# Tap products of two steps made together, signal products behind the inverse ones, and four store rooms instead of six

## The chip, the cores and the metric

The kernel runs on one core of a Trainium2 chip. The metric is the device time of one execution in microseconds (us); below it is given as the median of a few runs, with their spread.

## The reference

Two branches work on the same input x of 2048 rows and 512 columns, and a gate mixes them. All of it is fp32.

```python
g = sigmoid((x * gate_w).sum(-1, keepdims=True))
K = einsum("dn,dnl,dn->dl", C, exp(dt * A * l), dt * B).real   # taps, 512 x 2048
y = irfft(rfft(pad(x)) * rfft(pad(K)))[:, :2048] + x * Dskip   # long convolution
b = gelu(x @ w1 + b1) @ w2 + b2                                # 512 -> 1792 -> 512
out = g * y + (1 - g) * b
```

## The kernel before

The program has two parts. The function `front` makes the gate, nearly all of the dense branch b and the first stage of two Fourier transforms, that of the signal x and that of the taps K; a planner with a table of due times sets its order. Its results lie in DRAM (`tu_d` for the signal, `tk_d` for the taps, `od` for the dense branch) and in rooms in SBUF. The change does not touch `front`.

The function `conv`, which the change edits, runs from about 399 us of the span to its end. Its order is written out by hand: each engine does its instructions in the order of the program. Its loop has 16 steps; step s treats the two rows of frequencies 2s and 2s+1.

- `taps(s)` (line 1283 through `pair`): second stage for the taps, two products with 128 rows and 64 columns of weights into each of two PSUM banks, `pk0` and `pk1`. ScalarE then copies each bank into a room `k` (line 1291). There is one bank of each name, so that the next `taps` waits for the copies.
- `signal(s)` (also line 1283): the same for the signal, with weights of 64 rows and 64 columns, into two of four banks `pu0` to `pu3`.
- `product(s)` (lines 1305 to 1310): six VectorE operations multiply the two spectra, from the `pu` banks and the `k` rooms into `v`.
- `inverse(s)` (line 1322): the inverse transform's first stage, again with 64 by 64 weights, into the banks `pa0` and `pa1`, of which there is one each.
- `turn(s)` (lines 1328 to 1330): ScalarE copies `pa0` and `pa1` into two of the store rooms `sa`, and SyncE's queue stores these in DRAM (`t_d` in the profile). After each fourth step, GpSimd's queue loads the turned data of four steps back (line 1342); where a load's target is still in use it is held and issued later (line 1411).
- `fetch(n)` (line 1255): SyncE's queue loads a tap row of 256 KB. `consts` (line 1247) loads constants, and `matrices` (lines 1268 and 1269) lets ScalarE make weights `f` from them, four operations in each odd step up to step 11. `dense` (line 1355) loads 512 KB of the dense branch in steps 4 to 8, 10 and 12, and `gated` (line 1361) scales two tiles of it on ScalarE in steps 10 to 15.

In step s, TensorE's order before is: signal(s+1), taps(s+2), inverse(s). Behind the loop stand what is left of the dense branch (`rest`, lines 1372 to 1374) and the last stage (line 1445). In the texts below, T(s), S(s), I(s) and D(s) stand for taps(s), signal(s), inverse(s) and product(s).

Of the kernel before, what the change touches and what calls it, by code (L numbers as in the profile page):

```python
# [17 lines left out]
P = 128  # L18
L = 2048
D = 512  # L20
# [71 lines left out]
N_ATTIC, N_LOFT, N_TK = 11, 8, 8  # L92
# [295 lines left out]
def gated_mix(  # L388
# [37 lines left out]
    def places(attic, loft, den, shed):  # L426

        rooms = [attic[:, k] for k in range(N_ATTIC)] + [loft[:, k * D : k * D + D] for k in range(N_LOFT)]
        return [den[:, k] for k in range(N_DEN)] + rooms + [shed[:, k] for k in range(32 - N_DEN - N_ROOM)]
# [799 lines left out]
    def conv(pool, ps, late, attic, loft, den, shed, io, ahead):  # L1229


        def tiles(n, shape, nm):
            return [pool.tile(shape, F32, name=f"{nm}{k}", bufs=1) for k in range(n)]

        ks, zs = (tiles(n, [P, D], nm) for n, nm in ((4, "k"), (2, "z")))
        f1s = tiles(2, [P, 4, 64], "f1")
        cc3 = tiles(1, [P, 384], "cc")
        g1t = pool.tile([P, 2, 64], F32, name="g1t", bufs=1)
        t3 = tiles(3, [P, 8, D], "t3")
        vs = tiles(4, [P, D], "v")  # L1240
        sas = tiles(6, [P, D], "sa")
        us = places(attic, loft, den, shed)
        ko = k0_order()
        c4s, mats, t2s = {}, {}, {}
# [1 line left out]
        def consts(m):  # L1246
            nc.sync.dma_start(ccs[m % 4], c2[m])
            c4s[m] = ccs[m % 4]

        def fetch(n):  # L1250
            if 16 <= n < 24:
                t2s[n] = t3[0][:, n - 16]
            else:
                t2s[n] = rows[:, n % N_TK]
            nc.sync.dma_start(t2s[n], tk_d[ko[n]])

        def matrices(m):

            cc = c4s[m]
            f = cc[:, 0:256].rearrange("p (n k) -> p n k", n=4)  # L1260
            f1 = f1s[m % 2]
            for a in (0, 64):
                re, im = slice(a, a + 32), slice(a + 32, a + 64)
                if m < 2:
                    nc.gpsimd.tensor_scalar(f1[re], f[im], -1.0, None, ALU.mult)
                    nc.gpsimd.tensor_copy(f1[im], f[re])
                else:
                    nc.scalar.mul(f1[re], f[im], -1.0)
                    nc.scalar.copy(f1[im], f[re])
            mats[m] = (f, f1), cc[:, 256:384].rearrange("p (s k) -> p s k", s=2)  # L1270
# [3 lines left out]
        def pair(s, r, c, out):  # L1274

            for i in range(2):
                n = 2 * s + i
                if r:
                    w, x = mats[n // 4][0][c][:, n % 4], t2s[n]
                else:  # L1280
                    h = slice(64 * c, 64 * c + 64)
                    w, x = mats[n // 4][0][0][h, n % 4], us[n][h]
                nc.tensor.matmul(out[64 * i : 64 * i + 64], w, x, start=True, stop=True)  # L1283

        def taps(s):
            fac[s] = []
            for c in range(2):
                pk = ps.tile([P, D], F32, tag=f"pk{c}", name=f"p2k{s}{c}", bufs=1)
                pair(s, 1, c, pk)
                k = ks[2 * c + s % 2]  # L1290
                nc.scalar.copy(k, pk)
                fac[s].append(k)

        def signal(s):
            pus[s] = []
            for c in range(2):
                pu = ps.tile([P, D], F32, tag=f"pu{2 * (s % 2) + c}", name=f"p2u{s}{c}", bufs=1)
                pair(s, 0, c, pu)
                pus[s].append(pu)

        def product(s):

            (ur, ui), (kr, ki) = pus.pop(s), fac.pop(s)
            v = [vs[2 * i + s % 2] for i in range(2)]
            nc.vector.tensor_mul(v[0], ur, kr)
            nc.vector.tensor_mul(v[1], ur, ki)
            nc.vector.tensor_mul(zs[0], ui, ki)
            nc.vector.tensor_mul(zs[1], ui, kr)
            nc.vector.tensor_sub(v[0], v[0], zs[0])
            nc.vector.tensor_add(v[1], v[1], zs[1])  # L1310
            prod[s] = v

        def inverse(s):

            v = prod.pop(s)
            for i in range(2):
                n = 2 * s + i
                pas[n] = ps.tile([P, D], F32, tag=f"pa{i}", name=f"pa{s}{i}", bufs=1)
                r = slice(64 * i, 64 * i + 64)
                w = mats[n // 4][1][r, s % 2]  # L1320
                for c in range(2):
                    nc.tensor.matmul(pas[n][64 * c : 64 * c + 64], w, v[c][r], start=True, stop=True)  # L1322

        def turn(s):

            for n in (2 * s, 2 * s + 1):
                sa = sas[n % 6]
                nc.scalar.copy(sa, pas.pop(n))
                g, k = divmod(n, GROUP)
                nc.sync.dma_start(t4_d[g, :, k].rearrange("e c q d -> (c q) e d"), sa)  # L1330
                if k < GROUP - 1:
                    continue
                rows = t4_d[g].rearrange("e k c q d -> (e k c) q d")

                for h in (0, 4, 8, 16, 24) if g == 3 else (0, 8, 16, 24):
                    if h > (16, 8, 8, 24)[g]:
                        held.append((t3[h // 8 % 3][g:P:4], rows[:, h : h + 8]))
                        continue
                    on = nc.gpsimd if n < 31 else nc.scalar
                    e = h + (4 if g == 3 and h < 8 else 8)  # L1340
                    to = t3[h // 8 % 3][g:P:4] if h > 7 else den[g:P:4, h:e]
                    on.dma_start(to, rows[:, h:e])
# [4 lines left out]
        def dense(k, on):  # L1347

            q = (*HERE, *THERE).index(k)
            if q < 5:  # L1350
                mos[k] = attic[:, 2 * q : 2 * q + 2]
            else:
                r = 2 * q - 10
                mos[k] = loft[:, r * D : (r + 2) * D].rearrange("p (s d) -> p s d", s=2)
            on.dma_start(mos[k], od[k])

        def gated(k):

            for i in range(2):
                z = mos[k][:, i]  # L1360
                nc.scalar.mul(z, z, gate[:, 1, 2 * k + i : 2 * k + i + 1])

        def rest(n):

            while late and n:
                s, h, l, w, wl = late.pop(0)
                first = s not in accs
                last = not any(e[0] == s for e in late)
                if first:
                    accs[s] = ps.tile([P, D], F32, tag=f"pu{s}" if s > 1 else f"pk{s}", name=f"acc{s}", bufs=1)  # L1370
                ss = slice(s % 2 * P, s % 2 * P + P)
                nc.tensor.matmul(accs[s], h[:, ss], w, start=first, stop=False)  # L1372
                nc.tensor.matmul(accs[s], h[:, ss], wl, start=False, stop=False)
                nc.tensor.matmul(accs[s], l[:, ss], w, start=False, stop=last)
                n -= 1
# [16 lines left out]
        signal(0)  # L1392
        signal(1)
        taps(0)
        taps(1)
        for s in range(16):

            for n in range(2 * s + N_TK + (2 if s else 0), 2 * s + N_TK + 4):
                if n < 24:
                    fetch(n if n < 16 else n + 8)  # L1400
            if s in (2, 4, 6, 8):
                consts(s // 2 + 3)
            if s % 2 and s < 13:
                matrices(s // 2 + 2)
            product(s)
            if 0 < s < 15:
                signal(s + 1)
            if s + 2 < 16:
                taps(s + 2)
            if s in (10, 11, 12):  # L1410
                nc.sync.dma_start(*held.pop(0))
            if s == 15:
                rest(N_REST)
            inverse(s)
            turn(s)
            if s in TIMES:
                dense((*HERE, *THERE)[TIMES.index(s)], nc.sync)
            if s > 9:
                gated(HERE[s - 10])
# [5 lines left out]
        for s in range(4):  # L1425
            m, i = 7 - s // 2, s % 2
            z, g = mos[m][:, i], gate[:, 1, 2 * m + i : 2 * m + i + 1]
# [9 lines left out]
        for k, m in enumerate(ORDER):  # L1437
# [10 lines left out]
            for i in range(2):  # L1448
                t = 2 * m + i
                z, g = mos[m][:, i], gate[:, 0, t : t + 1]  # L1450
# [32 lines left out]
    with (  # L1483
        tc.tile_pool(name="fp", bufs=2, reuse_waits="tile") as fp,
        tc.tile_pool(name="ps_f", bufs=2, space=PSUM, reuse_waits="tile") as ps_f,
    ):
        conv(fp, ps_f, late, attic, loft, den, shed, io, ahead)
# [66 lines left out]
```

## Time and profile before

| what | us |
|---|---|
| median of 3 runs | 495.22 (494.23 to 496.56) |
| the profiled execution, its own time | 495.36 |
| its span, first to last instruction | 493.6 |
| TensorE busy in the span | 481.9 (98%) |
| VectorE busy | 416.2 (84%) |
| ScalarE busy | 368.9 (75%) |

The span is what the trace covers; the time of the same execution is 1.8 us longer. Busy time of TensorE is modelled from pipelined instructions, so a busy TensorE is not one without waits. The granted TensorE clock is 0.998 of full speed over the span.

### The profile page before, as it was taken

Reading aid. Unit: us, or ns where it says so; the run is one execution under the profiler, and the core shown is the slowest. Engines: PE = TensorE matmul, PEld = TensorE weight load, DVE = VectorE, ACT = ScalarE, POOL = GpSimd, SP = SyncE. Lnnn points to the kernel's source line nnn. Section 1 sums busy time; section 2 is a strip of 40 time slices with the busy share of each in tenths; the row PEclk is TensorE's granted clock in tenths of the full one; section 3 lists DMA queues with packets and bytes.
Section 4 is the critical chain, followed back from the end, with each engine's and each line's share of the span. In section 5 each row is a group of like instructions: output and inputs, shape, how many; then the busy total and the mean of one; then the engine's idle time right before and its main releaser. Section 6 shows DMA issues by size and latency. Waiting matters only on the chain.

```text
span 493.6 us, 12103 instructions
## 1 busy us (share of the span) xinstructions
PE 481.9 (98%) x4782; PEld 374.7 (76%) x4782; DVE 416.2 (84%) x653; ACT 368.9 (75%) x686; POOL 66.8 (14%) x107
## 2 busy tenths in 40 slices
PE   8999999999999999999999999999999999999995
PEld 7888787898897898888887979888888943222651
DVE  6999989989999997999899595999981149999563
ACT  4999767899885899996777997577655358789523
POOL 1102020110102100220121101020201040100012
PEclk9999999999999999999999999999999999999999
DMA  8989992686699762999784858695698897999988
GB/s 309 350 298 305 322 207 67 168 247 199 103 241 228 254 154 101 227 280 280 148 194 72 213 118 217 167 224 170 131 287 220 179 318 272 310 404 417 402 269 333
DMA packets 83848, 116.05 MB, mean 235 GB/s; under 512 B 39900, under 2 KB 43504, under 8 KB 83248
## 3 DMA queue, kind: packets, MB, share of 16 engines
q1 hardware_dynamic: 73776, 87.59, 54.8%
q0 software_dynamic: 9152, 23.89, 23.0%
q10 hardware_dynamic: 864, 3.80, 2.4%
q8 instruction: 37, 0.61, 0.5%
q14 instruction: 19, 0.16, 0.1%
HBM read 65.97 MB, written 49.29 MB: 234 GB/s over the span
## 4 chain that ended last, share of the span: by engine, by line
PE 85%; ACT 6%; DVE 6%; issue 2%; POOL 0%; DVEq 0%; ACTq 0%; POOLq 0%
PE pk L837 12%; PE ph L1029 9%; PE acc L1088 9%; PE ph L1031 9%; PE ph L1030 9%; PE acc L1089 8%; PE acc L1090 8%; PE p2k L1283 6%; PE pa L1322 3%; PE pb L1445 3%; PE ph L517 3%; PE p2u L1283 2%; PE pk L1160 1%; PE acc L1372 1%; DVE y L812 1%
## 5 line engine op out<-in xcount | busy, mean ns | idle before, releaser
L1029 PE MATMUL ph<-xh,wh 128*128 128x256 f32 x432 | 123.3, 286 | 2.1 <-issue 1.2
L1031 PE MATMUL ph<-xh,wl 128*128 128x256 f32 x432 | 122.2, 283 | 0.0
L1030 PE MATMUL ph<-xlo,wh 128*128 128x256 f32 x432 | 122.1, 283 | 0.0
L1029 PEld LDWEIGHTS ph<-xh,wh 128*128 128x128 f32 x432 | 82.0, 190 | 8.9 <-issue 4.0
L1030 PEld LDWEIGHTS ph<-xlo,wh 128*128 128x128 f32 x432 | 82.0, 190 | 3.3 <-issue 1.3
L1088 PE MATMUL acc<-wh,hh 128*128 128x512 f32 x206 | 83.2, 404 | 0.1
L1031 PEld LDWEIGHTS ph<-xh,wl 128*128 128x128 f32 x432 | 82.0, 190 | 0.0
L1089 PE MATMUL acc<-wl,hh 128*128 128x512 f32 x206 | 81.1, 394 | 0.3 <-DVE wl L940 0.3
L1090 PE MATMUL acc<-wh,hl 128*128 128x512 f32 x206 | 80.5, 391 | 0.0
L1060 ACT ACTIVATE ph<-ph,b1t 128x256 f32<-128x256 f32 x112 | 50.4, 450 | 34.0 <-PE ph L1031 30.6
L643 DVE TENSOR_TENSOR loft<-den,shed 128x512 f32<-128x512 f32 (+2 forms) x48 | 67.0, 1396 | 0.2
L1073 DVE TENSOR_TENSOR hl<-ph,hh 128x512 fp32r<-128x512 f32 (+1 forms) x62 | 38.2, 618 | 30.2 <-ACT hh L1063 27.4
L837 PE MATMUL pk<-y,den 128*32 128x64 f32 x2048 | 61.6, 290 | 0.2 <-DVE y L823 0.2
L837 PEld LDWEIGHTS pk<-y,den 128*32 128x32 f32 x2048 | 57.2, 136 | 4.1 <-issue 2.2
L1088 PEld LDWEIGHTS acc<-wh,hh 128*128 128x128 f32 x206 | 38.7, 188 | 17.2 <-issue 8.6
L1090 PEld LDWEIGHTS acc<-wh,hl 128*128 128x128 f32 x206 | 38.7, 188 | 8.7
L1089 PEld LDWEIGHTS acc<-wl,hh 128*128 128x128 f32 x206 | 38.7, 188 | 6.4 <-DVE wl L940 0.6
L1063 ACT CAST hh<-ph 128x512 fp32r<-128x512 f32 (+1 forms) x62 | 33.1, 533 | 10.1 <-PE acc L1089 7.3
L644 DVE TENSOR_TENSOR den<-loft 128x256 f32<-128x256 f32 (+2 forms) x48 | 37.2, 775 | 0.2
L812 DVE TENSOR_TENSOR y<-y,loft 128x2048 f32<-128x2048 f32 x16 | 36.6, 2286 | 0.1
L737 DVE CUSTOM_DVE_ANT_0 phase<-phase 128x128 uint16<-128x128 uint16 (+1 forms) x64 | 25.8, 403 | 0.5
L1060 ACT ACT_TABLE_LOAD x20 | 25.7, 1283 | 0.3
(204 smaller groups left out, 862.8 us busy)
## 6 DMA issues: line engine op xcount, KB each, us to landing
tu_d<-attic SPq DMA_DIRECT2D x64, 128.0 KB, 4.7
tk_d<-sk SPq DMA_DIRECT2D x32, 256.0 KB, 5.6
t_d<-sa SPq DMA_DIRECT2D x32, 256.0 KB, 5.7
ahead<-tk_d SPq DMA_DIRECT2D x18, 256.0 KB, 3.7
attic<-in_xt_dram SPq DMA_DIRECT2D x16, 256.0 KB, 5.4
xh_d<-xh SPq DMA_DIRECT2D x8, 512.0 KB, 5.8
xl_d<-xlo SPq DMA_DIRECT2D x8, 512.0 KB, 7.9
attic<-in_xs_dram SPq DMA_DIRECT2D x16, 256.0 KB, 4.9
```

Of the source, the lines that this page charges most:

```text
L643: vec(4 * m, lambda: nc.vector.tensor_mul(t, z, b), due, [ka, "zz"], kt)
L812: v.tensor_mul(y[:, 0].rearrange("p (a b) c -> p a b c", a=2), e.rearrange("p (a b) c -> p a b c", a=2), cc,)
L837: nc.tensor.matmul(pks[q][32 * j : 32 * j + 32, :, gg], x[:, r, :, ch], y[:, r, :, ch], start=(r == 0), stop=(r == 1), skip_group_check=True,)
L1029: nc.tensor.matmul(p, h, xh[xk][:, d], start=(d == 0), stop=False)
L1030: nc.tensor.matmul(p, h, xlo[xk][:, d], start=False, stop=False)
L1031: nc.tensor.matmul(p, lo, xh[xk][:, d], start=False, stop=(d == 3))
L1060: nc.scalar.activation(phs[q][:, n], phs[q][:, n], AF.Gelu_apprx_tanh, bias=b1t[:, f : f + 1])
L1073: nc.vector.tensor_sub(lo, phs[q][:, 0:nf], hi.bitcast(F32))
L1088: nc.tensor.matmul(a, h, wh[1][w], start=start, stop=False)
L1089: nc.tensor.matmul(a, h, wl[1][w], start=False, stop=False)
L1090: nc.tensor.matmul(a, l, wh[1][w], start=False, stop=(j == 3))
L1283: nc.tensor.matmul(out[64 * i : 64 * i + 64], w, x, start=True, stop=True)
```

## The change

In each even step up to step 12 the taps of two steps are made, one behind the other, ahead of that step's inverse product; odd steps make none. The signal product of step s+2 comes behind the inverse product of step s. There are six `k` rooms instead of four, and four `sa` rooms instead of six. Tap rows are loaded four at a time, in steps 0, 2 and 4, the last eight up to two steps sooner. The tiles `t3` change places with `cc` and `g1t`.

```diff
--- before.py
+++ after.py
@@ -1232,13 +1232,13 @@
         def tiles(n, shape, nm):
             return [pool.tile(shape, F32, name=f"{nm}{k}", bufs=1) for k in range(n)]
 
-        ks, zs = (tiles(n, [P, D], nm) for n, nm in ((4, "k"), (2, "z")))
+        ks, zs = (tiles(n, [P, D], nm) for n, nm in ((6, "k"), (2, "z")))
         f1s = tiles(2, [P, 4, 64], "f1")
+        t3 = tiles(3, [P, 8, D], "t3")
         cc3 = tiles(1, [P, 384], "cc")
         g1t = pool.tile([P, 2, 64], F32, name="g1t", bufs=1)
-        t3 = tiles(3, [P, 8, D], "t3")
         vs = tiles(4, [P, D], "v")
-        sas = tiles(6, [P, D], "sa")
+        sas = tiles(4, [P, D], "sa")
         us = places(attic, loft, den, shed)
         ko = k0_order()
         c4s, mats, t2s = {}, {}, {}
@@ -1287,7 +1287,7 @@
             for c in range(2):
                 pk = ps.tile([P, D], F32, tag=f"pk{c}", name=f"p2k{s}{c}", bufs=1)
                 pair(s, 1, c, pk)
-                k = ks[2 * c + s % 2]
+                k = ks[3 * c + s % 3]
                 nc.scalar.copy(k, pk)
                 fac[s].append(k)
 
@@ -1324,7 +1324,7 @@
         def turn(s):
 
             for n in (2 * s, 2 * s + 1):
-                sa = sas[n % 6]
+                sa = sas[n % 4]
                 nc.scalar.copy(sa, pas.pop(n))
                 g, k = divmod(n, GROUP)
                 nc.sync.dma_start(t4_d[g, :, k].rearrange("e c q d -> (c q) e d"), sa)
@@ -1395,24 +1395,28 @@
         taps(1)
         for s in range(16):
 
-            for n in range(2 * s + N_TK + (2 if s else 0), 2 * s + N_TK + 4):
-                if n < 24:
-                    fetch(n if n < 16 else n + 8)
+            if s == 0:
+                for n in range(8, 12):
+                    fetch(n)
             if s in (2, 4, 6, 8):
                 consts(s // 2 + 3)
             if s % 2 and s < 13:
                 matrices(s // 2 + 2)
             product(s)
-            if 0 < s < 15:
-                signal(s + 1)
-            if s + 2 < 16:
+            if s % 2 == 0 and s < 14:
                 taps(s + 2)
+                taps(s + 3)
+                if s in (0, 2, 4):
+                    for n in range(12, 16) if s == 0 else range(2 * s + 20, 2 * s + 24):
+                        fetch(n)
             if s in (10, 11, 12):
                 nc.sync.dma_start(*held.pop(0))
             if s == 15:
                 rest(N_REST)
             inverse(s)
             turn(s)
+            if s < 14:
+                signal(s + 2)
             if s in TIMES:
                 dense((*HERE, *THERE)[TIMES.index(s)], nc.sync)
             if s > 9:
```

The order of TensorE's instructions, from I(8) on (`pa` is written by inverse products, `p2u` by signal products, `p2k` by tap products). Before:

```order
L1322 MATMUL pa_5018<-v_4661,ahead 64x512
L1322 MATMUL pa_5018<-v_4663,ahead 64x512
L1322 MATMUL pa_5021<-v_4661,ahead 64x512
L1322 MATMUL pa_5021<-v_4663,ahead 64x512
L1283 MATMUL p2u_5039<-loft,ahead 64x512 x2
L1283 MATMUL p2u_5042<-loft,ahead 64x512 x2
L1283 MATMUL p2k_5045<-t_4658,ahead 64x512 x2
L1283 MATMUL p2k_5049<-t_4658,f_4655 64x512 x2
L1322 MATMUL pa_5053<-v_4662,ahead 64x512
L1322 MATMUL pa_5053<-v_4664,ahead 64x512
L1322 MATMUL pa_5056<-v_4662,ahead 64x512
L1322 MATMUL pa_5056<-v_4664,ahead 64x512
```

After the change, from I(8) on:

```order
L1322 MATMUL pa_5026<-v_4663,ahead 64x512
L1322 MATMUL pa_5026<-v_4665,ahead 64x512
L1322 MATMUL pa_5029<-v_4663,ahead 64x512
L1322 MATMUL pa_5029<-v_4665,ahead 64x512
L1283 MATMUL p2u_5036<-loft,ahead 64x512 x2
L1283 MATMUL p2u_5039<-loft,ahead 64x512 x2
L1322 MATMUL pa_5053<-v_4664,ahead 64x512
L1322 MATMUL pa_5053<-v_4666,ahead 64x512
L1322 MATMUL pa_5056<-v_4664,ahead 64x512
L1322 MATMUL pa_5056<-v_4666,ahead 64x512
L1283 MATMUL p2u_5063<-loft,ahead 64x512 x2
L1283 MATMUL p2u_5066<-loft,ahead 64x512 x2
```

Between I(8) and I(9) stood a signal and a tap product; now a signal product stands there alone, and tap products come only behind I(9) and S(11).

ScalarE from the copies of step 10 on (`sa` from `pa` are those copies, `attic` are two scalings of the dense branch, `f` the weights that `matrices` makes, `k` the copies of tap products). Before:

```order
L1328 COPY sa_4667<-pa_5084 128x512
L1328 COPY sa_4668<-pa_5087 128x512
L1361 ACTIVATE attic<-attic,gate 128x512 x2
L1268 ACTIVATE f_4655<-cc_4656 32x256
L1269 COPY f_4655<-cc_4656 32x256
L1268 ACTIVATE f_4655<-cc_4656 32x256
L1269 COPY f_4655<-cc_4656 32x256
L1291 COPY k_4649<-p2k_5113 128x512
L1291 COPY k_4651<-p2k_5117 128x512
L1328 COPY sa_4669<-pa_5122 128x512
L1328 COPY sa_4670<-pa_5125 128x512
```

After the change, from the copies of step 10 on:

```order
L1328 COPY sa_4667<-pa_5092 128x512
L1328 COPY sa_4668<-pa_5095 128x512
L1361 ACTIVATE attic<-attic,gate 128x512 x2
L1268 ACTIVATE f_4657<-cc_4661 32x256
L1269 COPY f_4657<-cc_4661 32x256
L1268 ACTIVATE f_4657<-cc_4661 32x256
L1269 COPY f_4657<-cc_4661 32x256
L1328 COPY sa_4669<-pa_5122 128x512
L1328 COPY sa_4670<-pa_5125 128x512
L1361 ACTIVATE attic<-attic,gate 128x512 x2
L1291 COPY k_4650<-p2k_5148 128x512
L1291 COPY k_4653<-p2k_5152 128x512
```

The tap copies that stood between the weights and the next store copies are gone from there (they were done in step 10 ahead of these rows); the copies of the next tap products stand behind two sets of store copies, two sets of scalings and the weights.

SyncE's queue, from the loads of step 2 or 3 to the stores of step 5 (`ahead<-tk_d` are tap rows, `t_d<-sa` stores, `attic<-od` the dense branch). Before, from the loads of step 3:

```order
L1255 DMA ahead<-tk_d 128x512 x2
L1330 DMA t_d<-sa_4665 64x2x512
L1330 DMA t_d<-sa_4666 64x2x512
L1255 DMA ahead<-tk_d 128x512 x2
L1247 DMA ahead<-in_c_dram 128x384
L1330 DMA t_d<-sa_4667 64x2x512
L1330 DMA t_d<-sa_4668 64x2x512
L1355 DMA attic<-od 128x1024
L1255 DMA ahead<-tk_d 128x512 x2
L1330 DMA t_d<-sa_4669 64x2x512
L1330 DMA t_d<-sa_4670 64x2x512
```

After the change, from the loads of step 2:

```order
L1255 DMA ahead<-tk_d 128x512 x4
L1330 DMA t_d<-sa_4667 64x2x512
L1330 DMA t_d<-sa_4668 64x2x512
L1330 DMA t_d<-sa_4669 64x2x512
L1330 DMA t_d<-sa_4670 64x2x512
L1247 DMA ahead<-in_c_dram 128x384
L1255 DMA ahead<-tk_d 128x512 x4
L1330 DMA t_d<-sa_4667 64x2x512
L1330 DMA t_d<-sa_4668 64x2x512
L1355 DMA attic<-od 128x1024
L1330 DMA t_d<-sa_4669 64x2x512
L1330 DMA t_d<-sa_4670 64x2x512
```

Loads of two tap rows stood in steps 3, 4, 5 and 6 (the last behind these rows); now loads of four stand in steps 2 and 4, and stores take the same room again after two steps.

## Rows read from the trace of the kernel before

**Rows 1.** The page's busy times of each engine: us, share of the span, instructions.

```profile
PE 481.9 (98%) x4782; PEld 374.7 (76%) x4782; DVE 416.2 (84%) x653; ACT 368.9 (75%) x686; POOL 66.8 (14%) x107
```

**Rows 2.** The chain of waits in order of time: start, us, what.

```profile
412.21 0.86 PE p2u L1283 x8
...
473.67 13.91 PE pb L1445 x68
```

**Rows 3.** Timeline of VectorE (DVE), start and end of stage: start, us, what.

```profile
403.38 0.69 DVE L1305 TENSOR_TENSOR v<-p2u,k 128x512 f32<-128x512 f32 x1 [2.84 <-ACT k L1291]
...
410.84 0.69 DVE L1305 TENSOR_TENSOR v<-p2u,k 128x512 f32<-128x512 f32 x1
...
414.44 0.69 DVE L1305 TENSOR_TENSOR v<-p2u,k 128x512 f32<-128x512 f32 x1
...
454.67 0.69 DVE L1305 TENSOR_TENSOR v<-p2u,k 128x512 f32<-128x512 f32 x1 [0.25 <-PE p2u L1283]
...
458.41 0.69 DVE L1305 TENSOR_TENSOR v<-p2u,k 128x512 f32<-128x512 f32 x1
...
461.41 0.69 DVE L1310 TENSOR_TENSOR v<-v,z 128x512 f32<-128x512 f32 x1
```

**Rows 4.** Timeline of TensorE (PE) in steps 1 to 3: start, us, what.

```profile
411.12 1.09 PE L1322 MATMUL pa<-v,ahead 64*64 64x512 f32 x8
...
413.00 1.08 PE L1283 MATMUL p2k<-ahead 128*64 128x512 f32 x4
413.91 1.03 PE L1283 MATMUL p2k<-ahead,f 128*64 128x512 f32 x4
414.87 1.09 PE L1322 MATMUL pa<-v,ahead 64*64 64x512 f32 x8
415.78 1.04 PE L1283 MATMUL p2u<-attic,ahead 64*64 64x512 f32 x8
...
418.61 0.66 PE L1322 MATMUL pa<-v,ahead 64*64 64x512 f32 x4
```

**Rows 5.** Timeline of TensorE, start-up, and a signal product of step 14.

```profile
401.61 1.08 PE L1283 MATMUL p2k<-ahead 128*64 128x512 f32 x4
...
403.40 1.08 PE L1283 MATMUL p2k<-ahead 128*64 128x512 f32 x4
...
453.53 1.04 PE L1283 MATMUL p2u<-shed,cc 64*64 64x512 f32 x8
```

**Rows 6.** Timeline of ScalarE (ACT): start-up, step 2, and steps 10 to 12.

```profile
402.76 0.58 ACT L1291 COPY k<-p2k 128x512 f32<-128x512 f32 x1 [2.68 <-DMA t<-tk_d]
...
416.01 1.07 ACT L1328 COPY sa<-pa 128x512 f32<-128x512 f32 x2 [0.37 <-PE pa L1322]
...
445.98 1.07 ACT L1328 COPY sa<-pa 128x512 f32<-128x512 f32 x2 [0.39 <-PE pa L1322]
447.07 1.33 ACT L1361 ACTIVATE attic<-attic,gate 128x512 f32<-128x512 f32 x2
...
450.11 1.07 ACT L1291 COPY k<-p2k 128x512 f32<-128x512 f32 x2
451.07 1.09 ACT L1328 COPY sa<-pa 128x512 f32<-128x512 f32 x2
...
453.43 1.05 ACT L1291 COPY k<-p2k 128x512 f32<-128x512 f32 x2
```

**Rows 7.** DMA: SyncE's issues (start, us); single store landings; DMA share by stretch.

```profile
421.70 1.05 SPq L1255 DMA_DIRECT2D ahead<-tk_d  x2
...
424.12 1.18 SPq L1330 DMA_DIRECT2D t_d<-sa  x2
...
t_d<-sa SPq DMA_DIRECT2D x1, 256.0 KB, 5.9
...
t_d<-sa SPq DMA_DIRECT2D x1, 256.0 KB, 8.7
...
424.00:446.00 22.00, 22.00 (x144) 5.99 (x144) 22.00 (x38) 17.33 (x37) 2.75 (x5) 1.00 1.02 377
```

## The prediction

> **What bounds the kernel now.** I read the page's busy times first: TensorE is busy nearly throughout [rows 1], so the first question for any edit is what it does to TensorE's order. Then the chain of waits, in order of time: through the loop of `conv` it is made of `pa`, `p2u` and `p2k` pieces and little else; behind the loop come the rest of the dense branch and the last stage [rows 2]. In the steady part the inverse product starts at 411.12, 414.87 and 418.61: 3.745 us a step, 7.49 a pair of steps [rows 4]. VectorE stands close behind: its product starts at 410.84 and again at 414.44, 3.60 a step, back to back [rows 3]. So TensorE has at most 0.145 a step to give before VectorE binds. Over the whole loop: VectorE starts at 403.38, 16 steps of 3.60 and the last operation's overhang of 0.09 end at 461.07; in fact its last operation ends at 461.41 + 0.69 = 462.10 [rows 3]. No reordering that leaves the start and VectorE's work alone can win more than 1.0 us in this loop. Behind its last operation the span has 493.6 - 462.10 = 31.5 us, which the change leaves as it is.
>
> **The saving on TensorE.** A piece of four concurrent 64 by 64 products costs 0.86 in the chain [rows 2]; a tap product is two such halves. The first half behind a change of tile shape takes 0.91 (413.00 to 413.91), the one ahead of a change 0.96 (413.91 to 414.87) [rows 4]. A change thus costs 0.05 + 0.10 = 0.15, and a pair of steps has four of them before, two after: 0.30 saved per pair, 2.1 over seven pairs, of which VectorE would let 1.0 through. Three waits, all covered before, stand against it.
>
> **First wait: the single banks.** T behind T needs the `k` copy of the same bank: the first T starts at 401.61, the next at 403.40, so 1.79 instead of 1.72 [rows 5]. That eats little. I(s+1) now stands directly behind I(s) and S(s+2), and both inverse products write the same `pa0` and `pa1`. The copies start 1.14 after the inverse product (414.87 to 416.01) [rows 4, 6] and the two last 1.07 [rows 6]; TensorE goes on 0.06 after a copy ends (402.76 + 0.58 to 403.40) [rows 5, 6]. So I behind I takes 2.27, where I and S fill 1.72. Before, a tap product of 1.87 covered this. A pair is now: I and S to T 0.86 + 0.96 = 1.82, T to T 1.79, T to I 0.86 + 0.96 = 1.82, I to I 2.27; in all 7.70 instead of 7.49, **0.21 more per pair**. Not shown anywhere is whether I(s+1) can start usefully on one bank; then I to I would be 1.14 + 0.58 + 0.06 = 1.78, the pair 7.21, and VectorE's 7.20 would bind. I take both banks, since the second bank's products end the piece.
>
> At the start T(3) now stands ahead of I(0): T at 401.61 + 3 x 1.79 = 406.98, I(0) at 408.80, I(1) at 411.07, as before (411.12). Five pairs on, I(11) is at 411.07 + 5 x 7.70 = 449.57 and I(10) 2.27 ahead of it, at 447.30.
>
> The Trainium skill has a rule on this too (TensorEngine Tiling, PSUM Bottleneck): tiling makes TensorE faster but not the emptying of PSUM, so that the copies may become the limit. Read as throughput it gives no loss before step 10: ScalarE's tap copies (451.07 - 450.11 = 0.96 for two), store copies (447.07 - 445.98 = 1.09) and weights (450.11 - 447.07 - 1.33 = 1.71) [rows 6] sum to 2 x 0.96 + 2 x 1.09 + 1.71 = 5.81 per pair, below 7.20, and the sum would be the rival with a gain below. What I expect is the latency of a single bank, which binds although ScalarE idles.
>
> **Second wait: ScalarE's order in steps 10 to 12.** From step 10 on each step adds two scalings. Between the copies of I(10) and the first tap copy of T(14) ScalarE now has, in order: store copies, scalings, four weights, which last 450.11 - 445.98 = 4.13; store copies and scalings, 453.43 - 451.07 = 2.36 [rows 6]; in all 6.49. The copies start at 447.30 + 1.14 = 448.44, so T(14)'s first tap copy starts at 454.93. TensorE starts T(14) at 449.57 + 1.82 = 451.39, and its bank is ready 1.15 later (401.61 to 402.76) [rows 5, 6], at 452.54. The copy is 2.39 late; T(15) waits for its bank, and behind T(15) on TensorE's queue I(12) and S(14), for which VectorE waits. T(15) starts at 454.93 + 0.58 + 0.06 = 455.57, I(12) at 457.39, S(14) at 458.25. The product starts 1.14 behind S (453.53 to 454.67) [rows 3, 5]: D(14) at 459.39, D(15) at 462.99, its last operation ends 3.69 later (458.41 to 462.10) [rows 3], at 466.68. That is **4.58 later than before**. Bounds: with one-bank starts I(11) comes 1.0 sooner and so does all behind it, 3.6; with the same scalings delayed by half a microsecond more, 5.1.
>
> **Third wait: four store rooms.** A store copy now needs the store of two steps before to have landed, 7.1 us after that copy's end (7.70 less 0.58). The DMA engines are full from 424 to 446 (share 1.02, 377 GB/s) [rows 7], and step 4's stores, issued as a pair from 424.12, land 5.9 and 8.7 us later [rows 7]. After the change I(4) is at 411.07 + 7.70 + 5.43 = 424.20 and its second store is issued at about 426.6. Ahead of it stand the same three loads of turned data (issued 0.2 to 0.5 later) and, of tap rows, 28 to 31; before, 26 and 27 stood there, at 421.70 [rows 7]. Two rows more at 256 KB / 377 GB/s = 0.70 each: the store that landed at 424.7 + 8.7 = 433.4 lands at about 435.1 (an estimate from these rows). I(6) is at 431.90, its second copy wants to start at 433.54 and waits 1.6; that shifts I(7), which needs the bank, and all behind it by **1.7**. Bounds: 0, if the store lands 5.9 after its issue, as its neighbour did; 3.2, if all four rows stand ahead of it. Later store copies: step 7's is already delayed by the same 1.7, and step 8's comes 1.7 later while the queue has two loads less to move from step 5 on; I count nothing.
>
> **What costs nothing.** Six `k` rooms are what two taps in advance need. The stores of step 0 now stand behind eight tap rows, the last of which waits for T(3); T(3) is done before I(0), so they wait for I(0) alone, and without that cover would be late by the 1.8 of one T. The moved `cc` lies where the dense branch's weights lay, whose last product is ahead of T(0), at 401.61 [rows 5], in TensorE's order. Loads 24 to 31 are used from T(12) on, 20 us later. Less backlog at the end of the DMA queue helps nobody: TensorE fills the tail [rows 2].
>
> **Sum.** 4.58 + 1.7 = 6.3 on the profiled execution's 495.36, less 0.14, by which the median of the runs lies below it: **501.5**.
>
> **Rivals.** (a) The store rooms do not bind; the other two waits do: 495.2 + 4.6 = 499.8. For it: the loads 28 and 29 go out before the turned data, and a store can land in 5.9. Against: full DMA engines. (b) The store rooms bind again and again up to step 10: another 1.6 in two later pairs, 504.7. Against: each delay gives the DMA engines time to work off what is queued, and loads of tap rows are over by then. (c) Not slower: the saved changes of tile shape count, I behind I costs 1.8, and ScalarE's late copies do not matter. TensorE would need 7.19 per pair and VectorE bind: 495.2 - 1.0 = 494.2. It decides at two places: I to I below 2.1 in the steady pairs, and T(14)'s first copy no later than 452.5. For it: both TensorE and VectorE have the work for 7.20 a pair. Against: 6.49 of ScalarE's work in one row cannot shrink.
>
> The Trainium skill states that a switch of tiling mode drains TensorE (TensorEngine Tiling, Key Properties). The 0.15 per change agrees with it; halving the changes is that rule's whole gain, and it is rival (c).
>
> **How the numbers follow.** What a measurement of this kernel can tell from no change is about 0.5%, 2.5 us. Forecast: 0.51; (a) 0.27; (b) 0.08; (c) 0.14, of which 0.03 beyond 0.5% through something that I don't see, as the loop alone has only 1.0 to give. The range runs from 495.2 + 3.6 - 0.4 = 498.4 (one-bank starts, no store wait, a little for the rounding of a dozen terms) to 495.2 + 5.1 + 3.2 = 503.5: it holds the forecast and (a), some 0.8. Slower 0.86, same 0.11, faster 0.03.
>
> **What would show it.** In the changed kernel: `pa` starts 2.27 apart within a pair and 7.7 from pair to pair; VectorE waits about 0.5 per pair for `p2u`; in step 12 about 4.2 from T(14) to T(15) with a `k` copy as releaser; ScalarE waiting for a store's landing in step 6; the last VectorE operation of the loop near 468.4, and 31.5 behind it. The prediction is wrong if `pa` pairs are closer, if the tap copies of step 12 aren't late, or if the tail shrinks.

## The result and the profile after

The changed kernel takes 502.56 us (median of four runs, 501.54 to 503.30), the kernel before beside it 495.18: a ratio of 1.0145 with a 95% interval of 1.0114 to 1.0177, so 1.45% slower. The profiled execution took 501.54 in all, with a span of 499.8.

The page's busy times, to be read against [rows 1]:

```profile
PE 485.8 (97%) x4782; PEld 376.2 (75%) x4782; DVE 416.3 (83%) x653; ACT 370.7 (74%) x686; POOL 66.8 (13%) x107
```

The counts of instructions are those of before, so the engines have the same work. TensorE's busy time is 3.9 us longer for the same instructions; it is modelled, so the added time is not read from it but from the starts on TensorE. The timeline of TensorE, a pair of steps and the two places with long waits (start, us, what, idle time before it and what ended it):

```profile
416.26 1.09 PE L1322 MATMUL pa<-v,ahead 64*64 64x512 f32 x8
417.17 1.04 PE L1283 MATMUL p2u<-attic,ahead 64*64 64x512 f32 x8
418.09 1.14 PE L1322 MATMUL pa<-v,ahead 64*64 64x512 f32 x6
419.00 0.59 PE L1283 MATMUL p2u<-attic,ahead 64*64 64x512 f32 x2
419.06 0.60 PE L1322 MATMUL pa<-v,ahead 64*64 64x512 f32 x2
419.43 1.08 PE L1283 MATMUL p2u<-attic,ahead 64*64 64x512 f32 x6
420.44 1.08 PE L1283 MATMUL p2k<-ahead,cc 128*64 128x512 f32 x4
...
422.23 1.08 PE L1283 MATMUL p2k<-ahead,cc 128*64 128x512 f32 x4
...
424.10 1.09 PE L1322 MATMUL pa<-v,ahead 64*64 64x512 f32 x8
...
435.81 1.30 PE L1322 MATMUL pa<-v,cc 64*64 64x512 f32 x6 [1.95 <-ACT sa L1328]
...
453.99 1.08 PE L1283 MATMUL p2k<-ahead,cc 128*64 128x512 f32 x4
...
458.10 1.08 PE L1283 MATMUL p2k<-ahead,cc 128*64 128x512 f32 x4 [1.85 <-ACT k L1291]
```

From I(2) at 416.26 to I(4) at 424.10 a pair takes 7.84, where before it took 7.49 [rows 4]. I(3) starts 1.83 behind I(2) with the products of its first bank, as soon as that bank is copied. Those of its second bank start when the second copy ends, 2.32 behind I(2) (418.58 in the trace, within the row of 418.09). So its last two products start only at 419.06 and six of S(5)'s eight at 419.43, and T(6) starts at 420.44, 4.18 behind I(2). I(7) at 435.81 waits for a store copy, T(15) at 458.10 for a tap copy: 4.11 after T(14). The timeline of ScalarE tells what held these two copies:

```profile
417.45 1.07 ACT L1328 COPY sa<-pa 128x512 f32<-128x512 f32 x2 [0.41 <-PE pa L1322]
...
435.17 1.24 ACT L1328 COPY sa<-pa 128x512 f32<-128x512 f32 x2 [2.50 <-DMA t_d<-sa]
...
451.00 1.07 ACT L1328 COPY sa<-pa 128x512 f32<-128x512 f32 x2 [0.44 <-PE pa L1322]
452.10 1.33 ACT L1361 ACTIVATE attic<-attic,gate 128x512 f32<-128x512 f32 x2
453.45 0.42 ACT L1268 ACTIVATE f<-cc 32x256 f32<-32x256 f32 x1
...
455.14 1.07 ACT L1328 COPY sa<-pa 128x512 f32<-128x512 f32 x2
456.24 1.33 ACT L1361 ACTIVATE attic<-attic,gate 128x512 f32<-128x512 f32 x2
457.48 1.05 ACT L1291 COPY k<-p2k 128x512 f32<-128x512 f32 x2
```

In step 6 the copy into a store room sat idle until an earlier store had landed. From step 10's store copies at 451.00 ScalarE worked without a gap, in the order of its queue, and came to T(14)'s tap copies 6.48 later (6.49 in the prediction). The timeline of VectorE shows where the loop begins and what this does to the products D:

```profile
402.87 0.69 DVE L1305 TENSOR_TENSOR v<-p2u,k 128x512 f32<-128x512 f32 x1 [2.84 <-ACT k L1291]
...
418.31 0.69 DVE L1305 TENSOR_TENSOR v<-p2u,k 128x512 f32<-128x512 f32 x1 [0.55 <-PE p2u L1283]
...
462.01 0.69 DVE L1305 TENSOR_TENSOR v<-p2u,k 128x512 f32<-128x512 f32 x1 [2.88 <-ACT sa L1328]
...
468.61 0.68 DVE L1310 TENSOR_TENSOR v<-v,z 128x512 f32<-128x512 f32 x1
```

A steady pair costs VectorE a wait of 0.55, and D(14) another 2.88. The profile puts the latter down to a store copy, which D(14) does not read; S(14) starts at 460.87, 1.14 ahead of D(14), the same 1.14 as between S(4) and D(4) (417.17 to 418.31), so it is S(14), behind the late T(15) and I(12), that D(14) waited for. The last operation ends at 469.29, before at 462.10 [rows 3]. From the first product's start (402.87, before 403.38 [rows 3]) the loop takes **66.42 instead of 58.72, 7.70 longer**. The span grew by 6.2 only: the loop began 0.51 sooner, and behind it lie 30.5 instead of 31.5. By windows, the last six microseconds of TensorE's work (columns: stretch, length, busy time of PE, PEld, DVE, ACT and POOL with counts, granted clock, DMA share, GB/s) in the kernel before:

```profile
481.60:487.60 6.00, 5.96 (x32) 2.01 (x28) 3.75 (x5) 3.82 (x6) 2.90 (x3) 1.00 1.03 419
```

and in the changed kernel:

```profile
488.90:494.90 6.00, 6.00 (x32) 2.01 (x28) 3.75 (x5) 3.82 (x6) 2.95 (x3) 1.00 0.84 339
```

Before, the DMA engines were full here (share 1.03), and the span went on for 6.0 us behind TensorE's last product, with the output's stores; after, the share was 0.84, and 4.9 were enough.

### The profile page after: what moved, and what is told of

The parts are those of the page before. It is cut to its first block, busy times and chain, and to the rows that moved or that the text cites. A ratio compares the mean times of both kernels' runs of the same rounds, so it can differ in the third digit from the quotient of the medians.

```text
span 499.8 us, 12087 instructions
## 1 busy us (share of the span) xinstructions
PE 485.8 (97%) x4782; PEld 376.2 (75%) x4782; DVE 416.3 (83%) x653; ACT 370.7 (74%) x686; POOL 66.8 (13%) x107
## 5 line engine op out<-in xcount | busy, mean ns | idle before, releaser
L1291 ACT COPY k<-p2k 128x512 f32<-128x512 f32 x32 | 18.6, 585 | 11.9 <-PE p2k L1283 8.2
```

## The experiments

In each, the kernel before ran beside on the same chip; ratios are to it. They are worked out from the single runs, not from the two medians, and differ from the quotient of the medians by up to 0.002. "Loop" is the time from the first product's start to the end of VectorE's last operation in the profiled execution, so it stands for one execution of each kernel.

**One wait taken away at a time.** Three kernels, each with one edit to the changed kernel, and one with all three. For six store rooms, the two `z` tiles give their place: two products are written over their own `k` rooms.

```diff
-        ks, zs = (tiles(n, [P, D], nm) for n, nm in ((6, "k"), (2, "z")))
+        ks = tiles(6, [P, D], "k")
-        sas = tiles(4, [P, D], "sa")
+        sas = tiles(6, [P, D], "sa")
-                sa = sas[n % 4]
+                sa = sas[n % 6]
-            nc.vector.tensor_mul(zs[0], ui, ki)
-            nc.vector.tensor_mul(zs[1], ui, kr)
-            nc.vector.tensor_sub(v[0], v[0], zs[0])
-            nc.vector.tensor_add(v[1], v[1], zs[1])
+            nc.vector.tensor_mul(ki, ui, ki)
+            nc.vector.tensor_mul(kr, ui, kr)
+            nc.vector.tensor_sub(v[0], v[0], ki)
+            nc.vector.tensor_add(v[1], v[1], kr)
```

Expected: 

> The changed kernel with six store rooms again; room for them is made by letting VectorE write its two middle products back into the k rooms, so that the z tiles go. Theory (store rooms are the third wait): the 2.5 us in which the store copies of step 6 wait for a landing go, T(8) to T(10) takes 7.84 as the other pairs do instead of 10.05, and the time falls by 2.2 to about 500.3. The other two waits stay: T(14) to T(15) near 4.1. Rival (the full DMA engines hold the kernel whatever the rooms, or the block of four loads does): the time stays within 0.5 of the changed kernel's 502.5.

Measured: 498.95, ratio 1.0063 (1.0039 to 1.0087). No copy waits for a landing any more, and the loop is 64.67, 1.75 shorter. The medians differ by 3.6, more than expected; the profiled executions differ by 2.2, but the changed kernel's was the fastest of its four and this one's the slowest. Rival (a)'s ground, that the store rooms do not bind, falls. Unforeseen was what the edit does to VectorE. Its timeline:

```profile
421.90 0.69 DVE L1305 TENSOR_TENSOR v<-p2u,k 128x512 f32<-128x512 f32 x1
422.50 0.68 DVE L1306 TENSOR_TENSOR v<-p2u,k 128x512 f32<-128x512 f32 x1
423.29 0.69 DVE L1307 TENSOR_TENSOR k<-p2u,k 128x512 f32<-128x512 f32 x1
```

The third operation starts 0.79 behind the second instead of 0.60: it overwrites the room that the second reads, and a product takes 3.80 instead of 3.60. A later run mends that.

The scalings of steps 10 and 11 made in steps 13 and 14:

```diff
-            if s > 9:
-                gated(HERE[s - 10])
+            for q in {12: (2,), 13: (3, 0), 14: (4, 1), 15: (5,)}.get(s, ()):
+                gated(HERE[q])
```

Expected: 

> The changed kernel with the scalings of steps 10 and 11 moved to steps 13 and 14, behind the last tap copies on ScalarE. Theory (ScalarE's order is the second wait): T(15) starts 1.8 behind T(14) instead of 4.1, and the time falls by 2.3 to about 500.2; the pairs before stay at 7.84, and the store wait of step 6 stays. Rival (T(15) or product 14 would be held by something else, a constant load or a store copy of steps 13 to 15 made late by the moved scalings): the time falls by under 1.

Measured: 500.95, ratio 1.0109 (1.0083 to 1.0134). T(14) to T(15) is 1.77, so the second wait is gone. But the median fell by 1.6 instead of 2.3, and the loop of the profile, 66.53, is no shorter: the profiled execution was the slowest of its four, 502.51, with a step 6 worse than the changed kernel's. TensorE's timeline there:

```profile
436.14 1.41 PE L1322 MATMUL pa<-v,cc 64*64 64x512 f32 x6 [2.77 <-ACT sa L1328]
...
437.76 1.06 PE L1283 MATMUL p2u<-attic,ahead 64*64 64x512 f32 x1
437.78 1.06 PE L1283 MATMUL p2u<-loft,ahead 64*64 64x512 f32 x1
```

and its windows, two of step 6 and the last six microseconds of TensorE's work, with the granted clock third from the end:

```profile
430.00:436.00 6.00, 3.37 (x24) 0.71 (x20) 5.47 (x10) 2.03 (x4) 0.00 (x0) 1.00 0.91 339
436.00:440.00 4.00, 3.85 (x16) 1.01 (x16) 2.22 (x4) 3.38 (x8) 0.00 (x0) 0.65 1.04 389
...
488.40:494.40 6.00, 6.00 (x33) 2.01 (x28) 3.75 (x5) 3.82 (x6) 2.95 (x3) 1.00 1.03 419
```

Behind a wait of 2.77 the granted clock was 0.65, that is mostly the lower of TensorE's two levels, 1.2 instead of 2.4 GHz, and a product of 0.59 took 1.06. From T(8) to T(10) 12.25 passed, where the changed kernel's profile has 10.05 with a wait of 1.95 and a clock of 1.00.

The second signal product of a pair moved between its two inverse products:

```diff
+            if s % 2 and s < 14:
+                signal(s + 2)
             inverse(s)
             turn(s)
-            if s < 14:
+            if s % 2 == 0 and s < 14:
                 signal(s + 2)
```

Expected: 

> The changed kernel with the signal product of each odd step ahead of that step's inverse product instead of behind it, so that two signal products stand between the two inverse products of a pair. Theory (the single pa banks are the first wait): the gap between the two inverse products is then filled by work of 1.72 and no longer held by the copies; a pair of steps falls from 7.84 to about 7.35 to 7.45, where the way from product over inverse, taps and signal back to product binds; the wait for store rooms grows by part of that, since step 6 comes sooner, and the time falls by 1 to 1.5, to about 501.2. Rival (the loss per pair is made by tap products that stand one behind the other): a pair stays at 7.8 and the time at 502.5.

Measured: 501.46, ratio 1.0119 (1.0096 to 1.0142). Steady pairs, from I to I, take 7.46 to 7.51 instead of 7.82 to 7.86; both long waits stay (1.60 and 1.85), and the loop is 64.96.

All three edits together:

Expected: 

> The changed kernel with all three edits at once: six store rooms with the z tiles gone, the scalings of steps 10 and 11 moved behind the last tap copies, and two signal products between the inverse products of a pair. Theory: the three waits are all that made the change slower, so the time comes back to within 1 us of the kernel before, 494.5 to 496, and with VectorE or the way round the loop at 7.3 to 7.45 a pair it can't be much better. Rival (something else, such as the pairing of tap products or the placing of loads, costs more): it stays above 497.5.

Measured: 495.89, ratio 1.0007 (0.9991 to 1.0024), loop 60.54. Without the three waits the new order is as fast as the old one, within the interval. It isn't faster, and VectorE's 3.80 was a suspect.

**From the other side.** The kernel before with only the four store rooms:

```diff
-        sas = tiles(6, [P, D], "sa")
+        sas = tiles(4, [P, D], "sa")
-                sa = sas[n % 6]
+                sa = sas[n % 4]
```

Expected: 

> The kernel before with four store rooms and nothing else changed. Theory: a store copy waits if the store of two steps before has not landed; in the trace of the kernel before, the stores of steps 4 to 8 land 7.5 to 9.6 after their copies, where two steps leave 6.9, so store copies of steps 6 to 10 wait by up to 2.7. A tap product stands between the inverse products there and covers 1.5 of each wait: 1 to 2.5 slower, 496 to 497.7. Rival (four rooms suffice as long as the loads and the order are those of before): within 0.5 of 495.2.

Measured: 498.15, ratio 1.0059 (1.0032 to 1.0086), above what was expected. From ScalarE's waits there (us in total, times, longest):

```profile
ACT sa L1328 <- DMA t_d<-sa: 9.2, 5, 4.5
```

Five copies wait for a landing, where in the loop of before none does; the loop is 2.1 longer than before, and the copies of step 15, one of which waits 4.5, come late for the last stage (behind the loop 33.2 instead of 31.5). So the store rooms bind by themselves, in either order.

The changed kernel with the tap rows 28 to 31 loaded in step 6 instead of step 4:

```diff
-                if s in (0, 2, 4):
-                    for n in range(12, 16) if s == 0 else range(2 * s + 20, 2 * s + 24):
-                        fetch(n)
+                for n in {0: range(12, 16), 2: range(24, 28), 6: range(28, 32)}.get(s, ()):
+                    fetch(n)
```

Expected: 

> The changed kernel with the loads of the last four tap rows (28 to 31) in step 6 instead of step 4. Theory (what stands ahead of step 4's stores in the DMA queue decides the store wait): the stores of step 4 land 2 to 3 sooner, the wait of the store copies of step 6 goes or falls below 0.5, and the time falls by 1.5 to 2 to about 500.8. Rival (the turned data alone make the stores late): the wait stays over 1.5 and the time at 502 to 502.6.

Measured: 500.24, ratio 1.0115 (1.0075 to 1.0155). Step 4's stores land 6.8 to 7.0 behind their copies instead of 9.2 to 9.4, and step 6 waits no more; step 8 does. ScalarE's timeline there:

```profile
440.76 1.22 ACT L1328 COPY sa<-pa 128x512 f32<-128x512 f32 x2 [1.03 <-DMA t_d<-sa]
```

The four rows do hold up the stores that are issued behind them. Moving them moves the wait and makes it smaller.

The kernel before with late scalings (the second edit above):

Expected: 

> The kernel before with the scalings of steps 10 and 11 moved to steps 13 and 14. Theory: ScalarE's order costs 0.25 there (T(14) waits for a tap copy), since each step of before has a tap product as cover, so 0 to 0.3 is to be had: 494.9 to 495.2, no change that can be measured. Rival (ScalarE's scalings hold the kernel before as well): over 1 faster.

Measured: 495.68, ratio 1.0008 (0.9980 to 1.0036). The old order has nothing to gain there that can be measured; the prediction had found that no reordering of this loop can win more than 1.0.

**A clean ladder.** Again six store rooms, but the in-place products in the other order, so that none overwrites what the operation just ahead reads:

```diff
-            nc.vector.tensor_mul(ki, ui, ki)
-            nc.vector.tensor_mul(kr, ui, kr)
-            nc.vector.tensor_sub(v[0], v[0], ki)
-            nc.vector.tensor_add(v[1], v[1], kr)
+            nc.vector.tensor_mul(kr, ui, kr)
+            nc.vector.tensor_mul(ki, ui, ki)
+            nc.vector.tensor_add(v[1], v[1], kr)
+            nc.vector.tensor_sub(v[0], v[0], ki)
```

Expected: 

> Six store rooms as in the run with six rooms, but the two products that go in place into the k rooms come in the other order, so that none overwrites what the operation just ahead of it reads. Theory: VectorE's six operations of a product lie back to back again (3.60 instead of 3.80); since pairs of about 7.8 are set by TensorE and ScalarE, nearly nothing comes of it: the six-room run's 498.95 less the 0.2 of the last product, about 498.8. Rival: the 0.2 per product were on the path: about 498.95 - 7 x 0.2 = 497.5 or less.

With late scalings too: 

> Six store rooms and the scalings of steps 10 and 11 moved to steps 13 and 14, in-place products in the better order; of the three waits only that for the single banks is left. Theory: T(14) to T(15) 1.8 instead of 4.1, no wait for a store's landing, pairs of 7.8 from beginning to end; 498.8 - 2.3 = 496.5, a loop (first product to last VectorE operation) of about 62. Rival: with the scalings moved, ScalarE is late elsewhere or the store rooms' wait comes back, 498 or more.

And with the second signal product ahead as well: 

> All three edits (six store rooms, late scalings, the second signal product of a pair ahead of the second inverse product) and the in-place products in the better order. If VectorE's 3.80 per product set the 7.34 to 7.52 of the pairs in the earlier run of all three, pairs become 7.2 to 7.3, the loop 59 to 59.5 and the time 494 to 494.7, about 1.2 below that run's 495.89 and a little below the kernel before. If TensorE's wait for the single banks sets them, pairs stay at 7.4 to 7.5 and the time at 495.5 to 496.

VectorE's timeline in the first of them shows 0.60 again behind the second operation:

```profile
421.11 0.68 DVE L1306 TENSOR_TENSOR v<-p2u,k 128x512 f32<-128x512 f32 x1
421.70 0.68 DVE L1307 TENSOR_TENSOR k<-p2u,k 128x512 f32<-128x512 f32 x1
```

| kernel | waits left | median | ratio to before | loop |
|---|---|---|---|---|
| changed | three | 502.56 | 1.0145 (1.0114 to 1.0177) | 66.42 |
| six rooms | first, second | 499.05 | 1.0088 (1.0056 to 1.0120) | 63.94 |
| and late scalings | first | 496.26 | 1.0023 (1.0002 to 1.0045) | 61.59 |
| and signal ahead | part of the first | 495.24 | 0.9999 (0.9982 to 1.0015) | 59.50 |
| before, beside them | none | 495.18 and 495.56 | 1 | 58.72 |

The second and third rows came out as their theories had it. The loop's 7.70 thus divide into 2.48 for the store rooms, 2.35 for ScalarE's order and 2.87 that are left with the first wait. Putting the signal product ahead takes 2.09 of these away; what the last 0.78 belong to is not shown. By time the third row is only 0.2% above before: its profile has 30.4 behind the loop instead of 31.5, and its loop began 1.9 sooner. Repairing the in-place order moved the six-room time by nothing that can be told (499.05 against 498.95): VectorE was not the bound there. With all three edits it shortened the loop, from 60.54 to 59.50, and VectorE's pairs from 7.52 to 7.44; the times, 495.89 and 495.24, can't be told apart by their intervals. TensorE's timeline of a pair in the third row's kernel, where only the first wait is left:

```profile
414.77 1.09 PE L1322 MATMUL pa<-v,ahead 64*64 64x512 f32 x8
...
418.88 1.08 PE L1283 MATMUL p2k<-ahead,cc 128*64 128x512 f32 x4
...
420.68 1.08 PE L1283 MATMUL p2k<-ahead,cc 128*64 128x512 f32 x4
...
422.54 1.09 PE L1322 MATMUL pa<-v,ahead 64*64 64x512 f32 x8
```

I to T 4.11, T to T 1.80, T to I 1.86: 7.77. The same in the fourth row's kernel:

```profile
415.39 1.09 PE L1322 MATMUL pa<-v,ahead 64*64 64x512 f32 x8
...
418.02 1.04 PE L1322 MATMUL pa<-v,ahead 64*64 64x512 f32 x8
418.99 1.08 PE L1283 MATMUL p2k<-ahead,cc 128*64 128x512 f32 x4
...
420.96 1.08 PE L1283 MATMUL p2k<-ahead,cc 128*64 128x512 f32 x4
...
422.83 1.09 PE L1322 MATMUL pa<-v,ahead 64*64 64x512 f32 x8
...
458.48 1.99 PE L1322 MATMUL pa<-v,cc 64*64 64x512 f32 x8 [2.22 <-DVE v L1310]
```

Here the banks are copied before I(3) wants them, and the pair is 7.44, where the order of before took 7.49. It stays above the 7.2 that VectorE could follow, as the second case of the expectation has it: of the 0.30 for shape changes, the single `k` banks take some back (T to T 1.97 instead of 1.79, the `k` copies standing behind I(3)'s store copies on ScalarE). The last row shows a new hole: with no tap or signal product left, TensorE stands idle for 2.22 ahead of I(14). By windows, the granted clock was 0.55 behind it:

```profile
458.00:461.00 3.00, 2.52 (x10) 0.85 (x11) 3.00 (x6) 2.33 (x5) 1.05 (x2) 0.55 1.06 409
```

**Filling the hole.** To the fourth row's kernel, rest products of the dense branch were added in step 14; in a second kernel step 15 has four groups instead of three (`rest(s - 11)`).

```diff
-            if s == 15:
+            if s > 13:
                 rest(N_REST)
```

Expected, three groups: 

> The kernel of the run before with all edits (495.24), and three groups of the dense branch's rest (nine products) made in step 14 ahead of I(14), where TensorE sat idle for 2.2 us and ran at the lower granted clock behind it. Theory: TensorE's idle time in front of I(14) goes, the granted clock stays at 1.00 from 455 to 470, and TensorE, which bounds all that follows, is done about 2.1 + 1.0 sooner: 492.2, ratio 0.994. Rival: the end is set by the last stores and loads behind D(15), which comes no sooner; then the time stays at 495.

Expected, four in step 15: 

> The same with four groups instead of three in step 15. Theory: between I(14) and I(15) three groups leave about 0.5 of TensorE idle, since I(15) waits for D(15); a fourth fills it: 0 to 0.5 below the run with three. Rival: the fourth delays I(15) and with it the last stores and loads, and the last stage waits for them: 0 to 0.7 above it.

Measured: 495.01, ratio 1.0002 (0.9980 to 1.0025), and 494.88, ratio 0.9982 (0.9960 to 1.0005); the difference of the two is not resolved. The theory of the first failed. The hole is gone and the clock is 1.00 from 455 to 470, as it said, yet the time is that of its rival. TensorE's waits in the first kernel from 440 on:

```profile
PE pb L1451 <- DMA den<-t_d: 1.4, 1, 1.4
PE pa L1322 <- DVE v L1310: 0.2, 1, 0.2
```

and the end of the second kernel's chain in order of time:

```profile
464.23 3.55 DMA t_d<-sa
467.93 3.05 DMA den<-t_d
471.11 13.97 PE pb L1451 x68
```

TensorE now comes early to the last stage and waits there for D(15)'s data, which go to DRAM and back: 1.4 in the first kernel, 0.5 in the second. And behind its last product the span goes on longer (6.6 in both profiles; 4.8 in that of the kernel without the added products). No kernel of this study is measurably faster than the one before.

## Why the prediction was right

Time and direction held, and all three waits were there. Two of the prediction's own signs came out against it, and the sum held in part because errors cancelled.

- **First wait, single banks: mechanism right, size too small.** The pair was put at 7.70 and took 7.84: 0.35 more than before instead of 0.21. T to T is 1.79 as predicted; T to I is 1.87 instead of 1.82, I to T 4.18 instead of 2.27 + 1.82 = 4.09. The sign named for it, `pa` starts 2.27 apart, failed: I(3) starts after 1.83. That is the term left open, a start on one bank, and it wins nothing, since the other half of I(3) starts after 2.32, when the second bank is copied, and half of S(5) behind that. With the other two waits gone the loop is 2.87 longer than before, where the prediction's sum without its late copy gives 4.58 - 2.39 = 2.19; the two-signal order takes 2.09 of it away. The Trainium skill states that tiling speeds up TensorE but not the emptying of PSUM, which may become the bottleneck (TensorEngine Tiling, PSUM Bottleneck). The trace agrees in one sense: the emptying set the pair, by the latency of single banks, while ScalarE was busy for 6.12 of the 7.84 us.
- **Second wait, ScalarE's order: right.** T(14) to T(15) was put at 4.18 and took 4.11; taking it away shortened the loop by 2.35, where the prediction's 4.18 less 1.79 is 2.39.
- **Third wait, store rooms: right in place, too small.** The second copy of step 6 was to come 1.6 late and shift the rest by 1.7. In the trace it is the first copy that waits: its store landed 9.2 us after its issue, not after 5.9 as before, at 435.07, and the second one's at 435.73 (435.1 in the prediction). The idle time is 2.50, TensorE's wait 1.95, and the two steps took 2.2 more than a steady pair. A second such wait, 2.33 in step 14, which the prediction did not count, costs TensorE nothing: I(15) starts 0.32 behind the start of the last product ahead of it, as before.
- **The sum.** The loop was put at 468.4 less 403.38 = 65.0 and took 66.42. Of the 1.4, six pairs at 0.14 are 0.84 and the store wait 0.5. Against it stand two errors the other way. The 31.5 behind the loop shrank to 30.5, which the prediction named as a sign of being wrong: "less backlog at the end of the DMA queue helps nobody" was not so. And the loop began 0.51 sooner, which is chance: in the profiles here, with the same work ahead of it, T(0) starts anywhere from 399.7 to 401.6. So the profiled execution's 501.54 meets the 501.5 by luck; it is the fastest of the four, and the median is 1.0 above the forecast.
- **The end of the span.** In all profiles here in which the DMA engines were full during TensorE's last six microseconds (share 1.02 or 1.03), the span went on for 6.0 to 6.6 behind its last product; where the share was 0.75 to 0.89, for 4.8 to 5.5. A longer loop alone doesn't empty them. The kernel with late scalings alone has a loop of 66.53 and ends with 6.3, behind a share of 1.03 (its last window above). What decides whether they are full there stays open.
- **The rivals.** That store rooms don't bind, and that they bind again and again up to step 10, fell by the two traces. The rival with no loss asked for I to I below 2.1 and T(14)'s copy not late. The first came about, 1.83, and was no sign of a gain, as the pair still took 7.84; the second did not, the copy coming 6.48 behind step 10's. Even with the waits cut away no kernel here is measurably faster than before: its pairs stay at 7.44, and what TensorE saved behind the loop came back as a wait for the last loads and as a longer end.

## What to carry over

Putting like products together to save changes of shape also puts together their claims on the same single bank and on one engine's queue: count for each bank how much work stands between its copy and its next writer, and for each late copy all that stands ahead of it on its engine. A cut in the number of buffers has to be weighed by the landing time under load (here up to 9.2 us from a store's issue), not by the shortest one (2.4). And before effort is spent on an order with less work, follow what is late next: filling a hole of 2.2 on TensorE won nothing here, as 1.4 came back as a wait for data and 1.8 behind its last product.

## What was not expected of the hardware

- **TensorE's clock behind a wait.** Idle times of 2.77 and 2.22 us were followed by stretches of granted clock 0.65 and 0.55, mostly at the lower level of 1.2 GHz, with products of 1.06 instead of 0.59 behind the first. The length of the wait alone does not decide it. After 2.20 it stayed at 1.00 from 458 to 461, in the kernel with all three edits, whose order on TensorE is that of the one with 2.22. After 1.66 it was 0.66 from 462 to 466 with six rooms and the better in-place order, and 1.00 with late scalings added; after 1.95 and 1.85 it stayed at 1.00 in the changed kernel's profile. The changed kernel's four runs had mean clocks of 1.000, 0.997, 0.994 and 0.995 at 501.54, 502.08, 503.04 and 503.30: the three below 1.000 were the longer ones. What a fall costs is read from two profiles with the same work: from I(14) over three groups of the dense branch to I(15) took 4.75 (458.48 to 463.23) behind the wait of 2.22, and 3.38 at full clock once the hole was filled (458.75 to 462.34, less I(15)'s own wait of 0.21), so 1.4. What decides whether the clock falls was not settled. A wait can thus cost more than its length.
- **VectorE's overlap of neighbours.** Operations of 0.68 start 0.60 apart, but 0.79 apart, so behind the end of the first, where the second overwrites an input of the first. Another order of the same operations brought 0.60 back.
